# Decode steps in a new order, and the distance and mask tables made on GpSimd

## The chip, the cores and the metric

One core of a Trainium2 chip runs the whole program. The metric is the device time of one execution in microseconds (us). Engines: PE (TensorE), with PEld its weight loads; DVE (VectorE); ACT (ScalarE); POOL (GpSimd); SP, which here only issues DMAs.

## The reference

Local attention, a gated product network and a cosine network, one behind the other.

```python
def _attn_ref(q, k, v, n_global, n_local):      # 4 batches, 8 heads, 768 x 64
    scores = scale * np.matmul(q, k.transpose(0, 1, 3, 2))
    is_global = pos[None, :] < int(n_global)                     # 8 columns
    is_local = (rel >= 0) & (rel < int(n_local))                 # 96 back
    keep = is_global | is_local
    dist = np.where(is_global & ~is_local, float(n_local), np.abs(rel))
    scores = scores - slopes[:, None, None] * dist[None, :, :]
    scores = np.where(keep, scores, -1e9)
    return softmax(scores) @ v
def _moe_ref(x, w1, w2, w3, w_out):             # x 3072 x 512
    return ((x @ w1) * (x @ w2) @ w3) @ w_out
def _moe2_ref(x, w_in, w_out):                  # w_in 512 x 2048
    h = x @ w_in
    return (h * np.cos(h)) @ w_out
```

The weights come as 64-bit floats. They are read as pairs of 32-bit words, and the kernel builds 32-bit floats of them.

## The kernel before

**Decoding.** 72 weight pieces of 128x512 lie in one list: 32 of `w3`, `wo1`, `w1`, `w2` in mixed order with 8 more of `w1`, `w2` behind them, then 16 of `in` (w_in) and 16 of `o2` (the last w_out). The generator `decoder()` walks the list in iterations; iteration i works on piece i and on the four pieces ahead of it in the pipeline. The steps of one piece are: the load (`w_load`, 512 KB, on SP), the words (`dec_words`, two ACT passes, L338 and L339), the shift (`dec_shift`, DVE, L343), the sign (`dec_sign`, DVE, L347) and the sum (`dec_sum`, DVE, L355), which is the last to read the raw words. Pieces of `w1` and `w2` are then split for the three-pass product: the high part is a cast (`w_hi`, ACT, L419), the low part a subtraction (`w_lo`, DVE, L423). Pieces of `in` go through `combos`, pieces of `o2` are stored to `late_w`. The raw buffers number six for the first 30 pieces (`EARLY`) and three from then on. So a later load waits until the sum of the piece three before it has been made.

**What sets the order.** Each engine runs its instructions in the order in which the code was written; the main loops call `decode(n)`, which lets the generator run to its n-th next `yield`. The code has 21 such turns ahead of the first stage.

**First stage: 16 chunks c.** Each chunk multiplies one piece of `w3` with one of `wo1` (`wmm`, L890) and takes one attention tile n = c-1 through its steps: scores (`a_scores`, L582), bias and minimum (`a_max`, L610, DVE), exponential (`a_exp`, L621, ACT), sum and reciprocal (`a_norm`, L631 and L634, DVE), scaling (L640, ACT; later L642, POOL), transposition of the tile before (`a_transpose`, L649), copy (`a_tcopy`), values (`a_values`, L676). In the first four chunks ACT also scales the two tables `d0` and `dist` into a bias for each head (`bias_heads`, L521, L522).

**Second stage: 96 slots sl**, 8 rounds of 12, with attention tile n = sl + 14. Slots 0 to 7 of a round make two products (`up`), slots 8 to 11 one (`down`). The results of `down` go out through the single buffer `x2t` (`down_out`, an ACT copy, L748, then `down_store`, L751, on SP), one slot later: in the slots 9, 10, 11 and, in the next round, 0. Loads of `qk` and `v` for the attention stand first in a slot on SP. The third stage (L1001 and on) has no decoding.

**Tables.** `biases()` makes `d0` and `dist` from two iotas and from the two scalars n_local and n_global, which are fetched to all partitions (`nraw`, issued on ACT's queue).

Of the kernel before, what the change touches and what calls it, by code (L numbers as in the profile page):

```python
# [13 lines left out]
ALU = mybir.AluOpType  # L14
# [9 lines left out]
LOC, GLB = 96, 8  # L24
# [24 lines left out]
FAR = 2.0 ** 120  # L49
# [220 lines left out]
def fused(ctx, tc, a_qk, a_v, w3p, wo1p, w1p, w2p, winp, wo2p, n_global, n_local, out):  # L270
    nc = tc.nc
# [55 lines left out]
    def dec_words(key):  # L327
        r = raws[key]
        if key[0] in ("w3", "wo1"):

            tag = dest[key]
            kw = {"bufs": 4} if tag == "Wb" else {}
            if key[1] % 2 == 0:
                two[key[0]] = wts.tile([128, 2, 512], F32, tag=tag, name=key[0], **kw)
            x = xs[key] = two[key[0]][:, key[1] % 2, :]
        else:
            x = xs[key] = ring(key, "x", [128, 512], F32)
        nc.scalar.activation(x, r[:, :, 1].bitcast(F32), ACTF.Copy, scale=2.0 ** -112)  # L338
        nc.scalar.activation(r[:, :, 0], r[:, :, 0].bitcast(U32), ACTF.Copy, scale=2.0 ** -29)  # L339
# [98 lines left out]
    def scalars():  # L438
        raw = misc.tile([128, 2, 2], I32, name="nraw")
        for i, src in enumerate((n_local, n_global)):  # L440
            nc.scalar.dma_start(
                out=raw[:, i, :], in_=src.bitcast(I32).to_broadcast([128, 2])
            )
        yield
        lo = misc.tile([128, 2], F32, name="nlo")
        hi = misc.tile([128, 2], F32, name="nhi")
        ng = misc.tile([128, 2], F32, name="nneg")
        nv = misc.tile([128, 2], F32, name="nval")
        nc.vector.tensor_copy(out=lo, in_=raw[:, :, 0])
        nc.vector.tensor_copy(out=hi, in_=raw[:, :, 1])  # L450
        nc.vector.tensor_scalar(ng, lo, 0.0, None, ALU.is_lt)
        nc.vector.tensor_tensor(out=hi, in0=hi, in1=ng, op=ALU.add)
        nc.vector.scalar_tensor_tensor(
            out=nv, in0=hi, scalar=4294967296.0, in1=lo, op0=ALU.mult, op1=ALU.add
        )
        yield nv

    def biases(tp):

        rel = tp.tile([128, 128 + LOC], I32, name="rel")  # L460
        col = tp.tile([128, 128], I32, name="col")
# [11 lines left out]
        nc.vector.tensor_copy(out=dist[:, :nr], in_=rel)  # L473
        nc.vector.tensor_copy(out=colf, in_=col)
        steps = scalars()
        next(steps)
        yield
        nv = next(steps)
        nl, ng = nv[:, 0:1], nv[:, 1:2]
        yield nv  # L480
        nc.vector.tensor_scalar(lt[:, :nr], dist[:, :nr], nl, None, ALU.is_lt)
        yield
        nc.vector.scalar_tensor_tensor(
            out=keep[:, :nr], in0=dist[:, :nr], scalar=0.0, in1=lt[:, :nr],
            op0=ALU.is_ge, op1=ALU.mult,
        )
        yield
        nc.vector.tensor_scalar(gl, colf, ng, None, ALU.is_lt)
        yield
        nc.vector.tensor_copy(out=keep[:, nr:], in_=gl[:, :GLB])  # L490
        yield

        nc.vector.tensor_tensor(out=tmp, in0=gl, in1=keep[:, :128], op=ALU.mult)
        yield
        nc.vector.tensor_tensor(out=gl, in0=gl, in1=tmp, op=ALU.subtract)
        yield
        nc.vector.scalar_tensor_tensor(
            out=tmp, in0=dist[:, :128], scalar=nl, in1=gl, op0=ALU.subtract, op1=ALU.mult
        )
        yield  # L500
        nc.vector.tensor_tensor(out=d0, in0=dist[:, :128], in1=tmp, op=ALU.subtract)
        yield
        nc.vector.tensor_tensor(out=tmp, in0=gl, in1=keep[:, :128], op=ALU.add)
        yield

        nc.vector.tensor_scalar(tmp, tmp, -1.0, -FAR, ALU.add, ALU.mult)
        yield
        nc.vector.tensor_scalar(keep, keep, -1.0, -FAR, ALU.add, ALU.mult)
        yield
        nc.vector.tensor_scalar(dist[:, nr:], colf[:, :GLB], 0.0, nl, ALU.mult, ALU.add)  # L510
        yield
        nc.vector.tensor_tensor(out=d0, in0=d0, in1=tmp, op=ALU.add)
# [268 lines left out]
    with tc.manual_schedule():  # L781
# [8 lines left out]
        for o in "3A3A3A3A3A3A3A3ABBBBBBBB":  # L790
# [3 lines left out]
            else:  # L794
                n, m = ups.pop(0)
# [7 lines left out]
        tp = pool("tp", 1, side="right")  # L803
        EARLY = 30
# [6 lines left out]
        def decoder():  # L811


            n = len(dec)
            for i in range(2):
                w_load(*dec[i][:2])
            for i in range(n + 5):
                fast = i < EARLY
                k = [dec[i - l][0] if 0 <= i - l < n else None for l in range(5)]

                def ready(stage, lag):

                    for l in range(4, lag - 1, -1):
                        if k[l] and (stage, k[l]) not in done:
                            done.add((stage, k[l]))
                            if stage == "sum" or k[l] in xs and isinstance(dest[k[l]], str):
                                yield k[l]

                if fast and i + 2 < EARLY:
                    w_load(*dec[i + 2][:2])  # L830
                if k[0] and fast:
                    dec_words(k[0])
                if k[1]:
                    dec_shift(k[1])
                    yield
                for key in ready("sum", 2):
                    dec_sum(key)
                    yield
                for key in ready("hi", 3 if fast else 2):
                    w_hi(key, dest[key])  # L840
                for key in ready("lo", 4 if fast else 2):
                    w_lo(key, nc.vector)
                    yield
                if k[1]:
                    dec_sign(k[1])
                    yield
                if not fast:
                    for key in ready("sum", 1):
                        dec_sum(key)
                        yield  # L850
                    if k[1] and k[1][0] == "in" and k[1][1] % 2:
                        yield from combos(k[1][1] // 2)
                if EARLY <= i + 2 < n:
                    w_load(*dec[i + 2][:2])
                if k[0] and not fast:
                    dec_words(k[0])

        dest = {key: d for key, _, d in dec}
        done = set()
# [3 lines left out]
        def decode(n):  # L863
            for _ in range(n):
                next(steps_left, None)

        a_load_plain(0, nc.scalar)
        a_scores(0)
        nc.vector.memset(pt_ps, 0.0)
        steps_b = biases(tp)  # L870
        next(steps_b)
        make_identity(nc, ident)
        nv = dists = None
        for i in range(21):
# [4 lines left out]
            if i == 4:
                nv = next(steps_b)  # L880
            elif i >= 6:
                dists = dists or next(steps_b)
# [539 lines left out]
```

## Time and profile before

| what | value |
|---|---|
| three runs | median 1138.04 us (1134.91 to 1139.94) |
| profiled execution | 1136.57 us, of it the traced span 1134.7 us |
| granted TensorE clock, mean | 0.995 |
| PE busy | 1106.8 us (98%), 6034 matmuls |
| DVE busy | 777.9 us (69%) |
| ACT busy | 680.2 us (60%) |
| POOL busy | 81.5 us (7%) |
| DMA | 219.22 MB, mean 193 GB/s |

The 1.9 us between the execution and its span lie before the first and behind the last traced instruction. A busy share is an average over three stages; what a wait is worth is read in the stage where it stands.

### The profile page before, as it was taken

How to read it: one execution, taken by the hardware profiler on the slowest of the kernel's cores; microseconds unless marked ns; L12 is line 12 of the kernel's file. 1: busy time of each engine (PE TensorE's matmuls, PEld its weight loads, DVE VectorE, ACT ScalarE, POOL GpSimd, SP SyncE). 2: the span in 40 equal slices, each digit the busy share in tenths (PEclk: the TensorE clock that was granted, in tenths of full speed). 3: DMA queues.
4: the chain of work that ended last, by engine and by line, in shares of the span. 5: the costliest groups of instructions: out<-in, count | busy, mean ns of one | idle time of the engine just before them, and what ended most of it. 6: DMA issues, size and time to landing. Idle time of an engine off the chain costs nothing.

```text
span 1134.7 us, 17350 instructions
## 1 busy us (share of the span) xinstructions
PE 1106.8 (98%) x6034; PEld 957.3 (84%) x6034; DVE 777.9 (69%) x1661; ACT 680.2 (60%) x1370; POOL 81.5 (7%) x161
## 2 busy tenths in 40 slices
PE   5999999999999999999999999999999999999997
PEld 2455899999999999999999878888888888888886
DVE  7797666757667676896516588885677884777741
ACT  6897776756666666866624476654355562555531
POOL 0000001111111112122100001100000000000000
PEclk9899999999999999999999999999999999999999
DMA  8865355554555555776254736549375459474261
GB/s 279 250 223 162 123 183 168 176 170 160 178 159 165 189 178 186 265 244 204 59 176 140 274 128 233 213 167 367 129 299 189 136 197 381 152 283 167 75 234 65
DMA packets 86768, 219.22 MB, mean 193 GB/s; under 512 B 9616, under 2 KB 26256, under 8 KB 86672
## 3 DMA queue, kind: packets, MB, share of 16 engines
q1 hardware_dynamic: 86160, 217.70, 56.0%
q8 instruction: 50, 0.82, 0.3%
q14 instruction: 46, 0.38, 0.1%
q10 hardware_dynamic: 512, 0.32, 0.1%
HBM read 178.14 MB, written 39.85 MB: 192 GB/s over the span
## 4 chain that ended last, share of the span: by engine, by line
PE 88%; DVE 6%; ACT 3%; DMA 2%; issue 1%; ACTq 0%; SPq 0%; DVEq 0%
PE mm L432 32%; PE o_ps L432 23%; PE h_ps L432 19%; PE x_ps L676 4%; PE mm L890 4%; PE pt_ps L649 2%; PE pt_ps L651 1%; PE s_ps L594 1%; PE s_ps L590 1%; PE s_ps L582 1%; DVE x L347 1%; DMA nraw<-in_n_global 1%; DVE x L355 1%; DMA raw<-in_w3p 1%; DMA v<-in_a_v 1%
## 5 line engine op out<-in xcount | busy, mean ns | idle before, releaser
L432 PE MATMUL o_ps<-o,g 128*128 128x512 f32 x960 | 223.3, 389 | 0.0
L432 PEld LDWEIGHTS o_ps<-o,g 128*128 128x128 f32 x960 | 180.0, 188 | 37.5
L432 PE MATMUL mm<-xT,wA 128*128 128x384 f32 x768 | 148.5, 343 | 0.0
L432 PE MATMUL mm<-ab,W 128*128 128x384 f32 x768 | 147.1, 341 | 0.0
L432 PE MATMUL mm<-xT,wB 128*128 128x384 f32 x768 | 147.1, 341 | 0.0
L432 PE MATMUL h_ps<-T,piece 128*128 128x512 f32 x576 | 141.7, 389 | 0.1
L432 PEld LDWEIGHTS mm<-xT,wA 128*128 128x128 f32 x768 | 133.1, 190 | 2.2 <-issue 1.5
L432 PEld LDWEIGHTS mm<-ab,W 128*128 128x128 f32 x768 | 131.6, 188 | 2.7 <-issue 2.4
L432 PEld LDWEIGHTS mm<-xT,wB 128*128 128x128 f32 x768 | 131.7, 188 | 2.1 <-issue 2.1
L432 PEld LDWEIGHTS h_ps<-T,piece 128*128 128x128 f32 x576 | 107.9, 188 | 23.2 <-DVE gr L1234 0.5
L558 ACT CAST hh<-qk 128x720 fp32r<-128x720 f32 x74 | 58.8, 794 | 104.1 <-PE s_ps L594 95.9
L642 POOL TENSOR_SCALAR e<-e,st 128x232 f32<-128x232 f32 x148 | 74.5, 516 | 498.9 <-DVE st L634 438.4
L432 PE MATMUL h_ps<-B,piece 128*128 128x512 f32 x432 | 106.0, 389 | 0.0
L432 PEld LDWEIGHTS h_ps<-B,piece 128*128 128x128 f32 x432 | 81.0, 188 | 17.1 <-DVE vv L1234 0.4
L621 ACT ACTIVATE e<-e,top 128x232 f32<-128x232 f32 (+1 forms) x192 | 89.1, 466 | 3.4 <-DVE top L610 3.3
L610 DVE CUSTOM_DVE_ANT_0 e<-s_ps,bias 128x232 f32<-128x232 f32 (+1 forms) x192 | 65.2, 376 | 32.9 <-PE s_ps L594 28.5
L1126 ACT ACTIVATE r<-r 128x1024 f32<-128x1024 f32 x48 | 51.0, 1062 | 33.3 <-DVE r L1120 33.3
L890 PE MATMUL mm<-wo,w 128*128 128x512 f32 x128 | 64.5, 638 | 4.8 <-DVE wo L355 4.8
L719 DVE TENSOR_TENSOR a_sb<-mm,a_sb 128x384 f32<-128x384 f32 x64 | 35.5, 554 | 46.5 <-PE mm L432 46.3
L1120 DVE SCALAR_TENSOR_TENSOR r<-kt,r 128x1024 f32<-128x1024 int32 x48 | 58.8, 1225 | 1.5
L659 ACT COPY pt<-pt_ps 128x512 f32<-128x512 f32 x80 | 46.7, 584 | 14.0 <-PE pt_ps L651 14.0
L1139 ACT CAST g<-gr 128x512 fp32r<-128x512 f32 x48 | 29.0, 621 | 42.1 <-PE o_ps L432 42.1
(136 smaller groups left out, 1681.5 us busy)
## 6 DMA issues: line engine op xcount, KB each, us to landing
piece<-a_s SPq DMA_DIRECT2D x84, 512.0 KB, 5.6
o<-o2s SPq DMA_DIRECT2D x80, 512.0 KB, 5.8
qk<-in_a_qk SPq DMA_DIRECT2D x74, 360.0 KB, 3.3
a_s<-ap SPq DMA_DIRECT2D x56, 256.0 KB, 2.3
v<-in_a_v SPq DMA_DIRECT2D x96, 128.0 KB, 3.1
raw<-in_w3p SPq DMA_DIRECT2D x16, 512.0 KB, 5.6
raw<-in_winp SPq DMA_DIRECT2D x16, 512.0 KB, 4.3
raw<-in_wo2p SPq DMA_DIRECT2D x16, 512.0 KB, 4.6
```

The lines of the kernel that those rows point to most:

```text
L432: nc.tensor.matmul(ps, lhsT=l, rhs=r, start=first and i + e == 0, stop=last and i == n - 1 and e == 2, skip_group_check=more,)
L558: nc.scalar.copy(out=hh[n], in_=qk_raw[n])
L610: nc.vector.tensor_tensor_reduce(out=es[n][:, e, :w], in0=sp[:, e, :w], in1=bias[:, 2 * p + e, :], scale=-0.125, scalar=3.0e38, op0=ALU.ad ...
L621: nc.scalar.activation(es[n][:, e, :w], es[n][:, e, :w], ACTF.Exp, bias=top[:, n, e:e + 1], scale=-1.0, accum_out=sts[n][:, 0, e:e + 1],)
L642: nc.gpsimd.tensor_scalar(x, x, st[:, 1, e:e + 1], 1.0, ALU.mult, ALU.mult)
L659: nc.scalar.copy(out=pts[n].rearrange("p a b c -> p (a b c)"), in_=pt_ps.rearrange("p a b c -> p (a b c)"),)
L676: nc.tensor.matmul(x[e * 64:(e + 1) * 64, i * 128:(i + 1) * 128], lhsT=vt[:kk, c, e * 64:(e + 1) * 64], rhs=pt[:kk, e, c, :], start=c == 0 ...
L719: nc.vector.tensor_tensor(out=t, in0=mm_ps.pop("b"), in1=t, op=ALU.mult)
L890: nc.tensor.matmul(W_ps[m], lhsT=wt["w3", c][:, m * 128:(m + 1) * 128], rhs=wt["wo1", k], start=k == 0, stop=k == M1 - 1,)
L1120: nc.vector.scalar_tensor_tensor(out=self.r, in0=self.kt, scalar=-c, in1=self.h if c == C1 else self.r, op0=ALU.mult, op1=ALU.add,)
L1126: nc.scalar.activation(self.r, self.r, ACTF.Sin, scale=0.5)
L1139: nc.scalar.copy(out=t[:, 0, :], in_=src[:, m, :])
```

## The change

It has five parts. (1) The tables: all of `biases()` and `scalars()` runs on GpSimd, in one go ahead of the decoding, and the scalars are fetched first on ACT's queue, ahead of the first attention tile. (2) From piece 30 on, load and words stand at the head of an iteration instead of its end. (3) There the low part is made one iteration after the cast instead of in the same one. (4) The first two pieces are summed right after their signs. (5) Chunk 15 takes 2 decode turns in its last call instead of 5, and slots from 48 on take 3 instead of 4, as the slots from 8 on do.

```diff
@@ scalars
-        nc.vector.tensor_copy(out=lo, in_=raw[:, :, 0])
-        nc.vector.tensor_copy(out=hi, in_=raw[:, :, 1])
...
+        nc.gpsimd.tensor_copy(out=lo, in_=raw[:, :, 0])
+        nc.gpsimd.tensor_copy(out=hi, in_=raw[:, :, 1])
...
@@ biases
-        nc.vector.tensor_scalar(lt[:, :nr], dist[:, :nr], nl, None, ALU.is_lt)
-        yield
-        nc.vector.scalar_tensor_tensor(
-            out=keep[:, :nr], in0=dist[:, :nr], scalar=0.0, in1=lt[:, :nr],
-            op0=ALU.is_ge, op1=ALU.mult,
-        )
...
+        pool = nc.gpsimd
+        pool.tensor_copy(out=dist[:, :nr], in_=rel)
+        pool.tensor_copy(out=colf, in_=col)
+        pool.tensor_scalar(keep[:, :nr], dist[:, :nr], 0.0, None, ALU.is_ge)
...
+        pool.tensor_scalar(lt[:, :nr], dist[:, :nr], nl, None, ALU.is_lt)
+        pool.tensor_tensor(out=keep[:, :nr], in0=keep[:, :nr], in1=lt[:, :nr], op=ALU.mult)
...
+        pool.tensor_tensor(out=dist, in0=dist, in1=keep, op=ALU.add)
+        yield nv, d0, dist
@@ decoder
-                if fast and i + 2 < EARLY:
+                if i + 2 < n and fast == (i + 2 < EARLY):
                     w_load(*dec[i + 2][:2])
-                if k[0] and fast:
+                if k[0]:
                     dec_words(k[0])
                 if k[1]:
                     dec_shift(k[1])
...
-                for key in ready("lo", 4 if fast else 2):
+                for key in ready("lo", 4 if fast else 3):
                     w_lo(key, nc.vector)
                     yield
...
-                if not fast:
+                if not fast or i <= 2:
                     for key in ready("sum", 1):
                         dec_sum(key)
                         yield
-                    if k[1] and k[1][0] == "in" and k[1][1] % 2:
-                        yield from combos(k[1][1] // 2)
-                if EARLY <= i + 2 < n:
+                if not fast and k[1] and k[1][0] == "in" and k[1][1] % 2:
+                    yield from combos(k[1][1] // 2)
+                if fast and i + 2 >= EARLY:
                     w_load(*dec[i + 2][:2])
-                if k[0] and not fast:
-                    dec_words(k[0])
@@ first stage
+        steps_b = biases(tp)
+        next(steps_b)
         a_load_plain(0, nc.scalar)
...
+        nv, *dists = next(steps_b)
         for i in range(21):
             decode(1)
...
-            decode(2 if c < 8 else {14: 1, 15: 5}.get(c, 3))
+            decode(2 if c < 8 else {14: 1, 15: 2}.get(c, 3))
@@ second stage
-                decode(2 if sl < 8 or sl >= 48 else 1)
+                decode(2 if sl < 8 else 1)
```

**Place one: the start, on DVE and POOL.** DVE's instructions before, from the wait for the scalars on (`w_135` and `wo_140` are the first two pairs of pieces):

```order
L449 CAST nlo<-nraw 128x2
L450 CAST nhi<-nraw 128x2
L451 TENSOR_SCALAR nneg<-nlo 128x2
L452 TENSOR_TENSOR nhi<-nhi,nneg 128x2
L453 SCALAR_TENSOR_TENSOR nval<-nhi,nlo 128x2
L343 TENSOR_SCALAR w_135<-w_135 128x512
L355 ISA wo_140<-raw,wo_140 128x1024
L481 TENSOR_SCALAR lt<-dist,nval 128x224
L347 SCALAR_TENSOR_TENSOR w_135<-raw,w_135 128x512
L483 SCALAR_TENSOR_TENSOR keep<-dist,lt 128x224
```

DVE now, from its second instruction on:

```order
L343 TENSOR_SCALAR w_161<-w_161 128x512
L347 SCALAR_TENSOR_TENSOR w_161<-raw,w_161 128x512
L355 ISA w_161<-raw,w_161 128x1024
L343 TENSOR_SCALAR wo_166<-wo_166 128x512
L347 SCALAR_TENSOR_TENSOR wo_166<-raw,wo_166 128x512
L355 ISA wo_166<-raw,wo_166 128x1024
L343 TENSOR_SCALAR w_161<-w_161 128x512
L347 SCALAR_TENSOR_TENSOR w_161<-raw,w_161 128x512
```

and POOL now, the last twelve of the 21 that depend on the scalars:

```order
L485 COPY keep<-gl 128x8
L486 TENSOR_TENSOR tmp<-gl,keep 128x128
L487 TENSOR_TENSOR gl<-gl,tmp 128x128
L488 TENSOR_SCALAR tmp<-dist,nval 128x128
L489 TENSOR_TENSOR tmp<-tmp,gl 128x128
L490 TENSOR_TENSOR d_113<-dist,tmp 128x128
L491 TENSOR_TENSOR tmp<-gl,keep 128x128
L492 TENSOR_SCALAR tmp<-tmp 128x128
L493 TENSOR_TENSOR d_113<-d_113,tmp 128x128
L494 TENSOR_SCALAR keep<-keep 128x232
L495 TENSOR_SCALAR dist<-colf,nval 128x8
L496 TENSOR_TENSOR dist<-dist,keep 128x232
```

All 21 instructions of the tables left DVE; POOL has 24 for them, 21 of which stand behind the scalars in one chain.

**Place two: DVE between the first and the second stage,** from the low parts of the last product of the first stage (`W`) to the first slot's bias. Before:

```order
L899 TENSOR_TENSOR W<-mm,W 128x512 x4
L423 TENSOR_TENSOR wB<-x,wB 128x512
L347 SCALAR_TENSOR_TENSOR x<-raw,x 128x512
L355 ISA x<-raw,x 128x1024
L343 TENSOR_SCALAR x<-x 128x512
L423 TENSOR_TENSOR wB<-x,wB 128x512
L347 SCALAR_TENSOR_TENSOR x<-raw,x 128x512
L355 ISA x<-raw,x 128x1024
L343 TENSOR_SCALAR x<-x 128x512
L423 TENSOR_TENSOR wB<-x,wB 128x512
L610 ISA e,top<-s_ps,bias_89 128x232
```

Now:

```order
L875 TENSOR_TENSOR W<-mm,W 128x512 x4
L347 SCALAR_TENSOR_TENSOR x<-raw,x 128x512
L355 ISA x<-raw,x 128x1024
L343 TENSOR_SCALAR x<-x 128x512
L423 TENSOR_TENSOR wB<-x,wB 128x512
L347 SCALAR_TENSOR_TENSOR x<-raw,x 128x512
L355 ISA x<-raw,x 128x1024
L592 ISA e,top<-s_ps,bias_89 128x232
```

Six decode instructions stand there instead of nine. The first sum (L355) is that of the `w2` piece 5; the load of the `w1` piece 7 waits for it, and ACT's words of that piece now stand ahead of the first slot's exponential.

**Place three: SP in two slots of a round's end with `o2` pieces.** Before (slots 70 and 71):

```order
L537 DMA qk<-in_a_qk 128x720
L551 DMA v<-in_a_v 128x256
L359 DMA late_w<-x 128x512
L751 DMA x2s<-x2t 128x384
L325 DMA raw<-in_wo2p 128x1024
L537 DMA qk<-in_a_qk 128x720
L551 DMA v<-in_a_v 128x256
L359 DMA late_w<-x 128x512
L751 DMA x2s<-x2t 128x384
L359 DMA late_w<-x 128x512
```

Now (slots 69 to 72 each read like this):

```order
L519 DMA qk<-in_a_qk 128x720
L533 DMA v<-in_a_v 128x256
L325 DMA raw<-in_wo2p 128x1024
L733 DMA x2s<-x2t 128x384
L359 DMA late_w<-x 128x512
```

The raw load moved ahead of the store of `x2t`. It waits for the sum of the piece three before it, which DVE makes as the last decode step of the same slot.

## Rows read from the trace of the kernel before

**Rows 1.** Page, part 4: the chain that ended last, share by engine.

```profile
PE 88%; DVE 6%; ACT 3%; DMA 2%; issue 1%; ACTq 0%; SPq 0%; DVEq 0%
```

**Rows 2.** Waits of PE: engine, line, releaser; us in all, times, longest.

```profile
PE mm L890 <- DVE wo L355: 4.8, 1, 4.8
PE pt_ps L649 <- ACT e L640: 4.6, 2, 2.4
PE x_ps L676 <- DMA v<-in_a_v: 4.2, 3, 1.8
```

**Rows 3.** Waits of DVE for ACT's words.

```profile
DVE x L343 <- ACT x L338: 22.6, 28, 2.1
```

**Rows 4.** Timeline, ACT and PE, 20 to 34 us: start, us, instruction, [idle before].

```profile
20.79 0.31 ACT L521 ACTIVATE bias<-d 128x128 f32<-128x128 f32 x1 [0.72 <-DVE d L512]
21.70 0.40 ACT L522 ACTIVATE bias<-dist 128x232 f32<-128x232 f32 x1 [0.60 <-DVE dist L514]
...
29.10 0.67 ACT L338 ACTIVATE w<-raw 128x512 f32<-128x512 f32 x1 [0.79 <-DMA raw<-in_w3p]
...
33.16 5.54 PE L890 MATMUL mm<-wo,w 128*128 128x512 f32 x8
```

**Rows 5.** Windows: us, PE, PEld, DVE, ACT, POOL busy (x), PEclk, DMA share, GB/s.

```profile
20.00:30.00 10.00, 6.50 (x18) 2.68 (x16) 10.00 (x29) 7.89 (x23) 0.00 (x0) 1.00 0.90 265
```

**Rows 6.** Timeline, DVE: first and last of 19 table instructions behind the scalars.

```profile
10.35 0.17 DVE L449 CAST nlo<-nraw 128x2 f32<-128x2 int32 x1 [1.54 <-DMA nraw<-in_n_global]
...
21.28 0.39 DVE L514 TENSOR_TENSOR dist<-dist,keep 128x232 f32<-128x232 f32 x1
```

**Rows 7.** Groups of POOL by form: busy us, mean ns of one.

```profile
L642 POOL TENSOR_SCALAR e<-e,st 128x232 f32<-128x232 f32 x124 | 64.8, 535 | 451.8 <-DVE st L634 394.8 <-ACT pt L659 36.0 <-PE s_ps L594 12.2
L642 POOL TENSOR_SCALAR e<-e,st 128x128 f32<-128x128 f32 x24 | 9.7, 417 | 47.1 <-DVE st L634 43.6 <-ACT pt L659 3.5
L423 POOL TENSOR_TENSOR wB<-raw,wB 128x512 fp32r<-128x512 f32 x4 | 5.8, 1438 | 150.3 <-ACT wB L419 150.3
```

**Rows 8.** Timeline, POOL: the same pair twice.

```profile
453.46 0.90 POOL L642 TENSOR_SCALAR e<-e,st 128x232 f32<-128x232 f32 x2 [4.28 <-DVE st L634]
...
466.16 1.59 POOL L642 TENSOR_SCALAR e<-e,st 128x232 f32<-128x232 f32 x2 [6.17 <-DVE st L634]
```

**Rows 9.** DVE's sums, L355: ns min/median/max of one.

```profile
L355 DVE CUSTOM_DVE_ANT_0 x<-raw,x x48: 668/685/834, 48.8 to 525.3; 128x1024 uint16<-128x1024 uint16 x48
```

**Rows 10.** Timeline, PE, the first nine slots: scores of tiles 14, 21, 22.

```profile
103.19 1.05 PE L582 MATMUL s_ps<-hh 64*128 64x232 f32 x4
...
114.89 0.33 PE L649 MATMUL pt_ps<-ident,e 128*128 128x128 f32 x1 [2.43 <-ACT e L640]
...
152.71 1.05 PE L582 MATMUL s_ps<-hh 64*128 64x232 f32 x4
...
158.41 0.27 PE L590 MATMUL s_ps<-hh 128*128 128x232 f32 x1
```

**Rows 11.** Timeline, DVE, SP and ACT, end of the first stage.

```profile
103.52 2.48 DVE L899 TENSOR_TENSOR W<-mm,W 128x512 fp32r<-128x512 f32 x4 [0.61 <-ACT W L898]
...
107.99 0.33 SPq L325 DMA_DIRECT2D raw<-in_w1p  x1
...
112.37 0.49 ACT L621 ACTIVATE e<-e,top 128x232 f32<-128x232 f32 x1 [1.08 <-DVE top L610]
```

**Rows 12.** DMA issues, 90 to 130 us: KB each, median us to landing.

```profile
raw<-in_w1p SPq DMA_DIRECT2D x3, 512.0 KB, 3.5
```

**Rows 13.** Timeline, SP, ACT and PE, 505 to 516 us.

```profile
505.58 0.38 SPq L325 DMA_DIRECT2D raw<-in_wo2p  x1
506.05 0.38 SPq L751 DMA_DIRECT2D x2s<-x2t  x1
...
511.56 0.48 ACT L748 COPY x2t<-mm 128x384 f32<-128x384 f32 x1 [2.88 <-DMA x2s<-x2t]
...
515.52 0.66 PE L676 MATMUL x_ps<-pt,v 128*64 128x128 f32 x8 [1.83 <-DMA v<-in_a_v]
```

More of the change, by code (lines that the diff above doesn't have):

```diff
@@ L448, in scalars @@
         nv = misc.tile([128, 2], F32, name="nval")
-        nc.vector.tensor_copy(out=lo, in_=raw[:, :, 0])
-        nc.vector.tensor_copy(out=hi, in_=raw[:, :, 1])
-        nc.vector.tensor_scalar(ng, lo, 0.0, None, ALU.is_lt)
-        nc.vector.tensor_tensor(out=hi, in0=hi, in1=ng, op=ALU.add)
-        nc.vector.scalar_tensor_tensor(
-            out=nv, in0=hi, scalar=4294967296.0, in1=lo, op0=ALU.mult, op1=ALU.add
-        )
+        nc.gpsimd.tensor_copy(out=lo, in_=raw[:, :, 0])
+        nc.gpsimd.tensor_copy(out=hi, in_=raw[:, :, 1])
+        nc.gpsimd.tensor_scalar(ng, lo, 0.0, None, ALU.is_lt)
+        nc.gpsimd.tensor_tensor(out=hi, in0=hi, in1=ng, op=ALU.add)
+        nc.gpsimd.tensor_scalar(hi, hi, 4294967296.0, None, ALU.mult)
+        nc.gpsimd.tensor_tensor(out=nv, in0=hi, in1=lo, op=ALU.add)
         yield nv
@@ L472, in biases @@
         nr = 128 + LOC
-        nc.vector.tensor_copy(out=dist[:, :nr], in_=rel)
-        nc.vector.tensor_copy(out=colf, in_=col)
+        own = slice(0, 128)
         steps = scalars()
@@ L477, in biases @@
         yield
+        pool = nc.gpsimd
+        pool.tensor_copy(out=dist[:, :nr], in_=rel)
+        pool.tensor_copy(out=colf, in_=col)
+        pool.tensor_scalar(keep[:, :nr], dist[:, :nr], 0.0, None, ALU.is_ge)
         nv = next(steps)
         nl, ng = nv[:, 0:1], nv[:, 1:2]
-        yield nv
-        nc.vector.tensor_scalar(lt[:, :nr], dist[:, :nr], nl, None, ALU.is_lt)
-        yield
-        nc.vector.scalar_tensor_tensor(
-            out=keep[:, :nr], in0=dist[:, :nr], scalar=0.0, in1=lt[:, :nr],
-            op0=ALU.is_ge, op1=ALU.mult,
-        )
@@ L487, in biases @@
[L487 to L512, printed above, removed]
@@ L513, in biases @@
-        yield
-        nc.vector.tensor_tensor(out=dist, in0=dist, in1=keep, op=ALU.add)
-        yield d0, dist
+        pool.tensor_scalar(lt[:, :nr], dist[:, :nr], nl, None, ALU.is_lt)
+        pool.tensor_tensor(out=keep[:, :nr], in0=keep[:, :nr], in1=lt[:, :nr], op=ALU.mult)
+        pool.tensor_scalar(gl, colf, ng, None, ALU.is_lt)
+        pool.tensor_copy(out=keep[:, nr:], in_=gl[:, :GLB])
+        pool.tensor_tensor(out=tmp, in0=gl, in1=keep[:, own], op=ALU.mult)
+        pool.tensor_tensor(out=gl, in0=gl, in1=tmp, op=ALU.subtract)
@@ new lines, in biases @@
+        pool.tensor_scalar(tmp, dist[:, own], nl, None, ALU.subtract)
+        pool.tensor_tensor(out=tmp, in0=tmp, in1=gl, op=ALU.mult)
+        pool.tensor_tensor(out=d0, in0=dist[:, own], in1=tmp, op=ALU.subtract)
+        pool.tensor_tensor(out=tmp, in0=gl, in1=keep[:, own], op=ALU.add)
+        pool.tensor_scalar(tmp, tmp, -1.0, -FAR, ALU.add, ALU.mult)
+        pool.tensor_tensor(out=d0, in0=d0, in1=tmp, op=ALU.add)
+        pool.tensor_scalar(keep, keep, -1.0, -FAR, ALU.add, ALU.mult)
+        pool.tensor_scalar(dist[:, nr:], colf[:, :GLB], 0.0, nl, ALU.mult, ALU.add)
@@ L869, in fused @@
         nc.vector.memset(pt_ps, 0.0)
-        steps_b = biases(tp)
-        next(steps_b)
         make_identity(nc, ident)
-        nv = dists = None
+        nv, *dists = next(steps_b)
         for i in range(21):
@@ L878, in fused @@
                 a_load_v(0)
[L879 to L882, printed above, removed]
         W_ps = {}
```

## The prediction

> **What bounds the kernel now.** I read the chain that ended last first: 88% of it is PE, so an edit on DVE, ACT or SP can only pay where PE waits [rows 1]. Then the waits of PE, and the reader is to see how short that list is: 4.8 us for the first sum at the very start, 4.6 us for the scaled tile, twice, and 4.2 us for `v` loads, three times [rows 2]. Against it stand 22.6 us in 28 waits of DVE for ACT's words [rows 3]. The change takes most of those 28 away, but in nearly all of them PE had work, so they are no part of the sum. Three places are left, and I read the timelines there.
>
> The start, up to 33.16 us, where PE begins the fourth chunk and then works without a pause for some 60 us [rows 4]. What holds it back is ACT, which goes through its words in program order. It stood 0.72 us for `d0`, 0.60 us for `dist` and 0.79 us for a raw piece [rows 4].
>
> The first slots. From the scores of tile 14 to those of tile 22 pass 55.22 us, eight slots. The last of them, without values, takes 5.70 us [rows 10]. Two of the eight have values as well, some 1.5 us each (an estimate: 24 matmuls a slot, of which a group of eight took 0.66 us [rows 13], so 2.0 if none overlaps, and I take 1.5). So 55.22 - 45.6 - 3.0 = 6.6 us are lost, and 2.43 us of that is one wait, at 114.89 [rows 10].
>
> The slots with `o2` pieces, 1.33 of them a slot, where the three waits for `v` lie. The last is 1.83 us at 515.52. Just before it ACT stood 2.88 us for the store of `x2t`, which SP had issued right behind a raw load [rows 13].
>
> **The start: -1.0 us.** DVE loses 21 instructions, 19 of them behind the scalars, 0.17 to 0.39 us each, and with them the 1.54 us in which it stood for the scalars [rows 6]. DVE was busy in the whole of 20 to 30 us [rows 5], so raw loads, which wait for its sums, are issued earlier. Two things cap this. The DMA engines were at 0.90 in that window [rows 5]: in ten microseconds data can come 1.0 us earlier, no more. And ACT's waits there are 2.1 us in all [rows 4]. So the gain lies between 0 and 2.1 us if the tables come in time; I take 1.0, the nearer row.
>
> Do they? POOL's chain is not in the trace, so I build it from its three rows [rows 7]. One-input operations cost 0.42 us on 128 columns and 0.54 on 232, so about 0.27 us fixed. The two-input one took 1.44 us on 512 columns; less the fixed part that is 2.3 ns a column, so 0.56 us on 128, 0.78 on 224 and 0.80 on 232. Of the 21 instructions behind the scalars eight are tiny (2.2 us), five one-input (2.3), eight two-input (six at 0.56, one at 0.78, one at 0.80: 5.0). Together 9.5 us, `d0` 1.6 us ahead of `dist`. The scalars landed by 10.35 us as the last of three transfers on ACT's queue [rows 6]; now they are first. I put them at 7.5 us, with 5 and 10.3 as ends.
>
> POOL and DVE also get in each other's way. One pair of scalings took 0.90 us, the same pair 1.59 us in a stretch with two decode instructions of DVE beside it, and DVE's sums, 0.685 us at the median, reach 0.834 [rows 8, 9]. So one POOL instruction loses up to (1.59 - 0.90) / 2 = 0.35 us, 21 of them 7.3 us if DVE never pauses. It pauses while it waits for words, so I take half, 3.7 us. `dist` is then ready at 7.5 + 9.5 + 3.7 = 20.7 us, `d0` at 19.1. ACT comes to `d0` at 20.79 - 0.72 = 20.1 and to `dist` 0.3 us later, so it stands some 0.3 us instead of 1.3. That fits the 1.0.
>
> The Trainium skill speaks against this edit (SBUF — State Buffer, "SBUF: two separate sides"): the port pair that GpSimd and VectorE share is an exclusive lock, held for a whole instruction, and the loser blocks fully. The trace agrees that POOL waits [rows 8], but DVE's sums lost 0.15 us at most [rows 9], less than a third of the instruction that POOL ran; taken at its word, the rule makes the lock rival below of this term.
>
> The first two sums made at once cost and bring nothing: the first product now waits for the first tile's scores, whose load became the last of the three on ACT's queue, due by 10.3 us, and the products are early for ACT anyway. If that load came later than 12 us, the start would lose the difference.
>
> **The first slots: -1.3 us.** Six decode instructions instead of nine stand between the `W` low parts and the first slot's bias, so the bias of tile 14 comes some 2.5 us earlier on DVE. I don't count that for the wait at 114.89, because something else is late next. The `W` low parts end at 106.0 us [rows 11]. Behind them come one sign and one sum, 0.69 us each [rows 9]: 107.3. Only then can SP issue the raw load that before went out at 107.99 [rows 11], and one of 512 KB lands 3.5 us later [rows 12]: 110.9. Since words now stand early, ACT makes that piece's words ahead of the exponential of tile 14: three passes with the cast behind them, 0.67 us each [rows 4], so the exponential starts at 112.9. Before it started at 112.37 [rows 11]. So this wait stays. Of the other 4.2 us of the 6.6, which come from DVE waiting for words and casts, I take 30%, since ACT is as full as before. The ends are +0.5 (the wait a little longer, nothing else gained) and -5.5 us (load in time, nearly all gone).
>
> **The `o2` slots: -1.0 us.** Sixteen slots with one piece each take the place of twelve with 1.33. DVE has one step of 0.69 us less a slot, and a quarter of the weight bytes less goes ahead of `v`. That would take most of the three 1.4 us waits. But a raw load now stands ahead of the store of `x2t` on SP and waits for the last decode step of the same slot. Queued behind it are that store, the `late_w` store, `qk` and `v`. In slots 69 to 72 this happens four times in a row: store late, next `down_out` on ACT late, exponential late, sum late, next load late. One such wait was 2.88 us [rows 13]; PE's own slack swallows the first, and of the next three I let 3.2 us reach PE, with 0 and 9 (three times 3) as ends. 4.2 becomes 3.2.
>
> **Slots 11, 12, 35, 36, 59 and 60: +1.3 us.** The same store stands behind a raw load in slots 10 and 11, 34 and 35, 58 and 59. Two in a row are mostly swallowed; I take 0.4 us for each of the three pairs, with 0 and 4.5 us (1.5 each) for all as ends. The move of `late_w` and the later end of the decoding (slot 81 instead of 72) cost nothing: the last round's loads begin in slot 84.
>
> **Sum.** -1.0 - 1.3 - 1.0 + 1.3 = -2.0 us. The profiled execution took 1136.57 us, 1134.7 of it span; the change would make it 1134.6. It lies 1.5 us below the median of the three runs, so for a median I give 1138.04 - 2.0 = 1136.0 us.
>
> **Rivals.**
>
> *Clear gain, 0.31.* The early load lands ahead of ACT, and the stores of `x2t` find a free queue, so that the slots keep PE's pace: start -1.0, first slots -5.0, `o2` -4.0, pairs 0: -10 us, 1128.0. For it speaks that the DMA engines are far from full outside the start, and that the median landing is 3.5 us [rows 12], less than a slot's 5.70 [rows 10]. Against it, place three: the wait is for the sum, not for bandwidth.
>
> *The lock, 0.09.* Every POOL instruction and every decode instruction exclude each other wholly, from either side. POOL's 9.5 us then become DVE time as well, `dist` is ready at 10.3 + 9.5 + 7.3 = 27.1 us, 5.4 after the 21.70 of before [rows 4]; less the 0.79 us that ACT stood anyway, the start loses 4.6 instead of gaining 1.0: 1141.6. It decides from `dist` at 22 us on, one microsecond for one. By the rule of the Trainium skill (SBUF — State Buffer) quoted above it would come out so.
>
> *The chain of stores, slower, 0.10.* The mechanism of the `o2` term at its ends: 9 us of waits instead of 4.2 (+4.8), the three pairs at 4.5, start -1.0, first slots -1.3: +7.0, 1145.0. It decides when the store of `x2t` lands later than some 3 us into the next slot in each of the runs of slots; the 2.88 us wait shows that it can [rows 13].
>
> *It doesn't do what it says.* Words early means only that ACT, not DVE, waits for the raw piece. Then the first slots gain nothing: 1137.3, inside the forecast.
>
> **Chances.** The forecast has 0.50, its own range 1133 to 1140. 0.5% of the median, 5.7 us, is about what a measurement can tell. Faster by more (below 1132.3): the clear gain and a little of the forecast's edge, 0.33. Slower by more (above 1143.7): the chain and a little of the lock, 0.12. The rest, 0.55. The range for eight in ten is 1127 to 1143.5.
>
> **What would show it.** Start: POOL's last table instruction at 20 to 22 us, ACT's first bias within 0.5 us of 20.4, the fourth chunk's product at 32 us. First slots: a raw load at 107 to 108 us and the transposition of tile 14 still waiting 2 us or more; if that wait is gone, the first-slot term is wrong. `o2`: ACT waiting for `x2s` in slots 70 to 73, raw loads each at the end of their slot, and waits for `v` of some 3 us in all. A prediction that is wrong will most likely be so there: if ACT shows no wait for `x2s`, the clear gain is right, and if it shows one in slots 11, 35 and 59 that PE answers, the chain.

## The result, and the profile after

Six runs of the changed kernel have a median of 1145.47 us (1142.96 to 1146.50) against 1137.37 us (1134.91 to 1139.94) of the kernel before: ratio 1.0066, 95% interval 1.0048 to 1.0084. It became slower by 8 us, where 2 us less were forecast. The profiled execution took 1145.51 us, its span 1143.6 us.

Page of the changed kernel, part 4, which answers to [rows 1]:

```profile
PE 84%; DMA 5%; ACT 4%; DVE 3%; issue 2%; POOL 1%; SPq 0%; ACTq 0%; POOLq 0%; DVEq 0%
```

PE's share fell from 88 to 84% and that of transfers rose from 2 to 5%. Waits of PE and then of ACT in the changed kernel, which answer to [rows 2] (its line numbers behind the tables are 18 to 24 lower; us in all, times, longest):

```profile
PE s_ps L564 <- DMA hh<-in_a_qk: 11.5, 2, 10.6
PE pt_ps L631 <- POOL e L624: 5.5, 4, 1.7
PE pt_ps L631 <- ACT e L622: 5.2, 2, 2.9
PE x_ps L658 <- DMA v<-in_a_v: 2.0, 2, 1.7
...
ACT x2t L730 <- DMA x2s<-x2t: 30.7, 10, 5.2
```

Before, the first and the last of these rows were:

```profile
PE s_ps L582 <- DMA hh<-in_a_qk: 7.0, 2, 5.4
...
ACT x2t L748 <- DMA x2s<-x2t: 4.4, 2, 2.9
```

The row of PE is for attention tiles, above all the first one, for which PE now waits until 10.57 instead of 5.41 us. It was the longest in PE's list before, and [rows 2] left it out. The row of ACT is the one that grew most: nine of the ten waits for the store of `x2t`, 29.3 us, lie in the slots with decoding, where before there was one of 2.88 us [rows 13]; the tenth, of 1.4 us, comes later and was there before too. DVE's row of waits for the words of [rows 3] is gone from its list, and PE has new waits for POOL's scaling, four times.

**Where the time went.** PE starts the scores of every tile in the same place of its program. Their start, from the timelines of PE, splits the 8.6 us up to slot 81; the difference of two neighbouring columns is what a stretch cost.

| us at which PE starts the scores of tile | 3 | 14 | 22 | 28 | 52 | 76 | 86 | 95 |
|---|---|---|---|---|---|---|---|---|
| slot | first stage | 0 | 8 | 14 | 38 | 62 | 72 | 81 |
| before | 39.07 | 103.19 | 158.41 | 192.05 | 325.74 | 459.44 | 520.85 | 571.65 |
| changed | 40.20 | 104.33 | 158.17 | 193.57 | 329.07 | 464.97 | 521.47 | 580.28 |
| changed less before | +1.13 | +1.14 | -0.24 | +1.52 | +3.33 | +5.53 | +0.62 | +8.63 |

So: start +1.1, first slots -1.4, three pairs of slots +1.8, +1.8 and +2.2, slots 62 to 72 -4.9, slots 72 to 81 +8.0. Behind slot 81 another 0.3 us (spans 1143.6 and 1134.7).

**The chain of stores.** Timeline of the changed kernel, SP, ACT, DVE and PE in slots 71 to 74 (start, us, instruction, [idle before]):

```profile
516.73 0.39 SPq L733 DMA_DIRECT2D x2s<-x2t  x1
...
525.78 0.33 SPq L325 DMA_DIRECT2D raw<-in_wo2p  x1
526.20 0.38 SPq L733 DMA_DIRECT2D x2s<-x2t  x1
...
521.39 0.48 ACT L730 COPY x2t<-mm 128x384 f32<-128x384 f32 x1 [3.67 <-DMA x2s<-x2t]
521.77 0.49 ACT L603 ACTIVATE e<-e,top 128x232 f32<-128x232 f32 x1
...
524.79 0.17 DVE L613 TENSOR_SCALAR st<-st 128x2 f32<-128x2 f32 x1
...
525.08 0.67 DVE L355 CUSTOM_DVE_ANT_0 x<-raw,x 128x1024 uint16<-128x1024 uint16 x1
...
530.51 0.48 ACT L730 COPY x2t<-mm 128x384 f32<-128x384 f32 x1 [5.02 <-DMA x2s<-x2t]
...
526.13 0.33 PE L631 MATMUL pt_ps<-ident,e 128*128 128x128 f32 x1 [1.68 <-POOL e L624]
...
526.91 3.70 PE L432 MATMUL mm<-xT,wA 128*128 128x384 f32 x12
...
539.50 0.66 PE L658 MATMUL x_ps<-pt,v 128*64 128x128 f32 x8 [1.74 <-DMA v<-in_a_v]
540.09 3.92 PE L432 MATMUL mm<-xT,wA 128*128 128x384 f32 x12
```

Read by time it is a ring. ACT's copy (521.39) comes late, so the exponential (521.77), DVE's step ahead of the reciprocal (524.79) and the sum behind it (525.08) come late. Only then can SP issue the raw load (525.78), and behind it the store (526.20). The next copy into the one buffer waits for that store and runs at 530.51: 9.1 us from copy to copy, where a slot takes 5.70 [rows 10].

PE answers twice. It waits 1.68 us for the scaled tile, and the next 12 matmuls take 3.70 us, where such a group takes 2.35 with the clock at its upper level. Window of the changed kernel over this wait (columns as in rows 5):

```profile
520.00:530.00 10.00, 8.32 (x40) 7.44 (x39) 5.16 (x14) 4.09 (x10) 1.15 (x2) 0.83 0.52 171
```

The granted clock of this stretch is 0.83, a mix of the two levels. Behind the wait for `v` at 539.50 it is the same again: 1.74 us of wait, and 3.92 us for the next 12 matmuls. The two waits and the 1.35 + 1.57 us of slow matmuls are 6.3 of the 8.0 us; the rest lies in the same two slots.

**The first slots.** Timeline of the changed kernel, SP, ACT and PE; it answers to [rows 11] and the wait in [rows 10]:

```profile
108.63 0.33 SPq L325 DMA_DIRECT2D raw<-in_w1p  x1
...
112.09 0.66 ACT L338 ACTIVATE x<-raw 128x512 f32<-128x512 f32 x1 [2.88 <-DMA raw<-in_w1p]
...
113.72 0.48 ACT L603 ACTIVATE e<-e,top 128x232 f32<-128x232 f32 x1
...
116.06 0.33 PE L631 MATMUL pt_ps<-ident,e 128*128 128x128 f32 x1 [2.35 <-ACT e L622]
```

ACT stood 2.88 us for the raw piece, made its words and its cast, and then the exponential. The wait of PE stayed (2.43 us before).

**The start.** Timeline of the changed kernel, POOL, DVE, PE and ACT:

```profile
8.64 0.18 POOL L449 CAST nlo<-nraw 128x2 f32<-128x2 int32 x1 [5.37 <-DMA nraw<-in_n_global]
...
22.49 0.73 POOL L496 TENSOR_TENSOR dist<-dist,keep 128x232 f32<-128x232 f32 x1
...
22.61 1.16 DVE L355 CUSTOM_DVE_ANT_0 w<-raw,w 128x1024 uint16<-128x1024 uint16 x1
...
12.41 9.83 PE L866 MATMUL mm<-wo,w 128*128 128x512 f32 x16
...
33.98 5.86 PE L866 MATMUL mm<-wo,w 128*128 128x512 f32 x8
...
6.02 0.66 ACT L338 ACTIVATE w<-raw 128x512 f32<-128x512 f32 x1 [2.51 <-DMA raw<-in_w3p]
```

The last row before:

```profile
4.40 0.66 ACT L338 ACTIVATE w<-raw 128x512 f32<-128x512 f32 x1 [0.67 <-DMA raw<-in_w3p]
```

`dist` was ready at 23.2 us, 14.6 us behind the first table instruction that depends on the scalars. ACT's words began 1.6 us later than before, and ACT came to the first bias at 21.81 us, where it had come at 20.07. The fourth chunk began at 33.98 instead of 33.16 us [rows 4].

### The profile page after: what moved, and what is told of

The parts are those of the page before. It is cut to its first block, busy times and chain, and to the rows that moved or that the text cites. A ratio compares the mean times of both kernels' runs of the same rounds, so it can differ in the third digit from the quotient of the medians.

```text
span 1143.6 us, 17329 instructions
## 1 busy us (share of the span) xinstructions
PE 1112.0 (97%) x6034; PEld 959.9 (84%) x6034; DVE 773.5 (68%) x1640; ACT 677.9 (59%) x1370; POOL 93.5 (8%) x185
## 4 chain that ended last, share of the span: by engine, by line
PE 84%; DMA 5%; ACT 4%; DVE 3%; issue 2%; POOL 1%; SPq 0%; ACTq 0%; POOLq 0%; DVEq 0%
PE mm L432 29%; PE o_ps L432 23%; PE h_ps L432 19%; DMA x2s<-x2t 3%; PE x_ps L658 3%; PE mm L866 3%; PE pt_ps L631 2%; ACT e L603 1%; PE pt_ps L633 1%; PE s_ps L564 1%; PE s_ps L576 1%; PE s_ps L572 1%; DMA raw<-in_w2p 1%; DMA nraw<-in_n_global 1%; DVE x L355 1%
## 5 line engine op out<-in xcount | busy, mean ns | idle before, releaser
L432 PE MATMUL mm<-xT,wA 128*128 128x384 f32 x768 | 151.7, 348 | 0.1
L432 PEld LDWEIGHTS mm<-xT,wA 128*128 128x128 f32 x768 | 136.0, 194 | 2.6 <-issue 1.5
L432 PEld LDWEIGHTS h_ps<-T,piece 128*128 128x128 f32 x576 | 108.0, 188 | 23.2 <-DVE gr L1210 0.5
L624 POOL TENSOR_SCALAR e<-e,st 128x232 f32<-128x232 f32 x148 | 71.8, 497 | 489.4 <-DVE st L616 428.6
L631 PE MATMUL pt_ps<-ident,e 128*128 128x128 f32 x192 | 46.9, 278 | 10.9 <-POOL e L624 5.5
L673 DVE TENSOR_TENSOR xT<-x_ps,xT 128x384 fp32r<-128x384 f32 x32 | 17.8, 557 | 55.0 <-ACT xT L672 55.0
```

The lines of the kernel that those rows point to most:

```text
L432: nc.tensor.matmul(ps, lhsT=l, rhs=r, start=first and i + e == 0, stop=last and i == n - 1 and e == 2, skip_group_check=more,)
L624: nc.gpsimd.tensor_scalar(x, x, st[:, 1, e:e + 1], 1.0, ALU.mult, ALU.mult)
L631: nc.tensor.transpose(pt_ps[:, e, 0, :], e_t[:, e, :128], ident)
L673: nc.vector.tensor_tensor(out=t[:, 1, :], in0=x, in1=t[:, 0, :].bitcast(F32), op=ALU.subtract)
```

## The experiments

Three theories on the slots: A, the harm goes through the one buffer of `x2t`; B, it goes through `qk` and `v`, which stand behind the waiting load on SP; C, slots with decoding are simply too full.

**The store on ACT's queue.**

```diff
-        nc.sync.dma_start(out=x2s[m, :, j * TB:(j + 1) * TB], in_=x2t.pop((j, m)))
+        nc.scalar.dma_start(out=x2s[m, :, j * TB:(j + 1) * TB], in_=x2t.pop((j, m)))
```

> The changed kernel, with the stores of x2t issued on ACT's queue instead of SP's, so that they no longer stand behind the raw load. Theory A (single buffer): the harm of the early load goes through x2t's one buffer, 5.7 us on PE in slots 11 to 14, 35 to 38 and 59 to 62 and 8.0 us in slots 72 to 75. Then all 13.7 us go: 1145.5 - 13.7 = 1131.8 us (1129 to 1135), and ACT's copy waits less than 3 us in all for x2s in the second stage instead of 29. Theory B (queue): the harm goes through qk and v, which still stand behind the waiting load on SP; then the time stays at 1142 to 1146 and PE still waits in slots 73 to 75.

Measured: 1133.20 us (1131.62 to 1134.84), ratio to the kernel before 0.9969 (0.9956 to 0.9982). Tile 95 starts at 566.32 us, 14.0 us ahead of the changed kernel, of which 13.2 lie in the pairs and behind slot 72 (5.8 and 7.4). Waits of PE and of ACT in this run:

```profile
PE x_ps L658 <- DMA v<-in_a_v: 0.4, 1, 0.4
...
ACT hh L540 <- DMA qk<-in_a_qk: 16.7, 11, 2.4
ACT x2t L730 <- DMA x2s<-x2t: 13.2, 4, 6.7
```

A holds, B falls. `qk` still comes late (16.7 us of ACT's waits against 7.7), and PE hardly feels it. In the slots where ACT had its 29.3 us of waits for `x2s`, none is left. One number of A was wrong: ACT waits 13.2 us for `x2s` in all, not under 3. One of the four waits ends at 577.03 us, in slot 83, the other three from 625.54 on, in and behind the last round; why the stores on ACT's queue are late there stays open.

**The raw load late.** Load behind the sums again, words early:

```diff
-                if i + 2 < n and fast == (i + 2 < EARLY):
+                if fast and i + 2 < EARLY:
                     w_load(*dec[i + 2][:2])
...
-                if fast and i + 2 >= EARLY:
+                if EARLY <= i + 2 < n:
                     w_load(*dec[i + 2][:2])
```

> The changed kernel, with the raw load from piece 30 on back at the end of an iteration (words stay at its head). Theories A (single buffer of x2t) and B (qk and v behind the load on SP) both expect 1131.8 us (1129 to 1136), since no load waits any more for a sum of its own slot. Theory C (the slots with decoding are simply too full on DVE or ACT): it stays at 1142 to 1146. If the time lies well above e1's, loads that come a slot later make ACT wait for raw pieces, which would stand in ACT's waits as more than 6 us for raw.

Measured: 1130.52 us (1129.66 to 1130.91), ratio 0.9940 (0.9926 to 0.9954). Tile 95 at 565.68. C falls: the place of the load alone is worth 14.6 us up to there between this run and the changed kernel. Waits of PE:

```profile
PE s_ps L564 <- DMA hh<-in_a_qk: 11.6, 2, 10.7
PE pt_ps L631 <- ACT e L622: 5.4, 2, 3.0
PE x_ps L658 <- DMA v<-in_a_v: 0.2, 1, 0.2
```

**The tables on DVE again** (parts of the diff on `scalars`, `biases` and their calls undone).

> The changed kernel with the tables on DVE and the scalars behind the first attention tile, as before the change. Theory D (the tables on GpSimd cost the start 0.8 us at the fourth chunk, 1.1 us from tile 3 on): the fourth chunk's product starts at 33.2 us again, tile 14's scores at 103.2. Rival E (the two sums made at once are what delays it): 33.9 and 104.3 stay. Time, one look: 1144.4 under D, 1145.5 under E.

Measured, one run: 1146.13 us, above both theories. The fourth chunk starts at 32.85 us, as D has it, but tile 3 at 39.67 and tile 14 at 103.79, halfway between D and E. So the tables on GpSimd cost about half of the 1.1 us, if anything; this isn't shown, since five runs with the changed start have tile 3 at 39.15 to 40.20 us. PE's rows of this run show why DVE alone doesn't cure it:

```profile
12.33 9.90 PE L888 MATMUL mm<-wo,w 128*128 128x512 f32 x16 [4.96 <-DVE wo L355]
```

The first product waits until 12.33 us for a sum of DVE, although the first two sums now stand early: DVE waits for the scalars ahead of the second one.

**The scalars fetched second,** tables on GpSimd:

```diff
-        steps_b = biases(tp)
-        next(steps_b)
         a_load_plain(0, nc.scalar)
         a_scores(0)
+        steps_b = biases(tp)
+        next(steps_b)
```

> The changed kernel with the scalars fetched behind the first attention tile on ACT's queue; the tables stay on GpSimd. Theory F (the fetch ahead is what costs: the DMA engines moved 180 to 190 GB/s at 2 to 5 us instead of 221 to 407): the fourth chunk's product comes at 33.3 us or earlier. Rival G (GpSimd's chain of 14.6 us from the scalars to dist sets the start): the scalars land about 1.7 us later, dist is ready at some 24.9 us instead of 23.2, and the product comes at 34.5 to 35.5 us.

Measured, one run: 1146.61 us. Rows of PE's timeline, and one of ACT's waits:

```profile
9.21 5.26 PE L866 MATMUL mm<-wo,w 128*128 128x512 f32 x8 [2.01 <-DVE wo L355]
...
32.22 0.68 PE L631 MATMUL pt_ps<-ident,e 128*128 128x128 f32 x2 [8.08 <-ACT e L622]
```

```profile
ACT bias L503 <- POOL d L493: 4.5, 1, 4.5
```

Both theories have a half. The fetch ahead did hold the first product: it now starts at 9.21 us instead of 12.41, since the first tile lands 4.5 us after its issue instead of 8.9. But POOL's chain then sets the start: `dist` is ready at 25.8 us, ACT stands 4.5 us for `d0`, the fourth chunk starts at 36.33, later than either theory had it, and tile 3 at 42.05, 1.9 us later than in the changed kernel. ACT's first words come at 4.59 us again, so it was the fetch ahead that had delayed them.

**One piece a slot, alone, in the kernel before.**

```diff
-                decode(2 if sl < 8 or sl >= 48 else 1)
+                decode(2 if sl < 8 else 1)
```

> The kernel before, with one edit of the change alone: slots from 48 on take 3 decode turns instead of 4, so one o2 piece a slot instead of 1.33. Theory H (the rate of pieces made the three waits for v): on PE some 5 us go between slots 60 and 72 (4.9 was gained there by the changed kernel), and no store chain comes, since loads stand at the end of an iteration: 1136.4 - 5 = 1131.5 us (1130 to 1133). Rival I (the early words or the later low parts did it): at most 1 us goes.

Measured: 1131.61 us (1131.51 to 1131.77), ratio 0.9956 (0.9940 to 0.9973). Tile 76 starts 0.2 us earlier than before, tile 86 5.6 us. H holds. The list of PE's waits has no row for `v` any more:

```profile
PE s_ps L582 <- DMA hh<-in_a_qk: 6.8, 2, 5.7
PE mm L890 <- DVE wo L355: 4.8, 1, 4.8
PE pt_ps L649 <- ACT e L640: 4.8, 2, 2.4
PE x_ps L676 <- ACT pt L659: 0.7, 2, 0.4
```

**The load late and 1.33 pieces a slot** (the edit of the run before, undone in the run with the load late).

> The changed kernel with the raw load at the end of an iteration (as in the run with the load late) and with 4 decode turns a slot from slot 48 on, as before the change. Theory H: the waits for v between slots 60 and 72 come back, 1130.5 + 5 = 1135.5 us (1134 to 1137). Rival I: it stays within 1 us of 1130.5.

Measured: 1139.81 us (1136.57 to 1143.72), ratio 1.0029 (1.0007 to 1.0050). H again in the main, but 4.3 us over its forecast of 1135.5. PE's three pauses ahead of the values come back in the same places (477.11, 495.66 and 514.75 us, 4.2 us in all), but only one of them ends with `v`; the other two end with ACT. What comes on top would be ACT's waits for raw pieces, 2.3 us in the run with the load late; that is not shown by itself:

```profile
ACT x L338 <- DMA raw<-in_wo2p: 11.2, 6, 5.2
```

With early words a load that is late holds ACT instead of DVE.

**Words late too** (part 2 undone whole).

```diff
-                if k[0]:
+                if k[0] and fast:
                     dec_words(k[0])
...
                 if EARLY <= i + 2 < n:
                     w_load(*dec[i + 2][:2])
+                if k[0] and not fast:
+                    dec_words(k[0])
```

> The changed kernel with its second part undone whole: from piece 30 on load and words both at the end of an iteration. Theory J (words early bring the 1.4 us of the first slots): PE's lead over the run with the load late is lost between the slots 0 and 6, 1.4 us, so 1132 us. Rival K (the later low parts and the shorter call in chunk 15 bring them): it stays at 1130.5, and the wait for tile 14's scaling gets shorter than 2.35 us, since the words of the w1 piece no longer stand ahead of its exponential. No store chain in either.

Measured: 1127.09 us (1126.71 to 1127.14), ratio 0.9916 (0.9899 to 0.9932). J falls outright: the early words did not bring the 1.4 us, they cost 4.4 in slots 0 to 7, and 3.4 in the time. K had the wait right, and its time 3.4 us too high. Tile 14 starts at 104.14 us and tile 22 at 153.50, 5.9 us less for these eight slots than before. PE's waits, and the window of 110 to 120 us:

```profile
PE s_ps L564 <- DMA hh<-in_a_qk: 11.2, 2, 10.6
PE pt_ps L631 <- ACT e L622: 2.7, 1, 2.7
PE x_ps L658 <- ACT pt L646: 1.3, 1, 1.3
```

```profile
110.00:120.00 10.00, 10.00 (x71) 8.93 (x71) 8.24 (x25) 8.79 (x24) 0.00 (x0) 1.00 0.67 172
```

Tile 14's wait is gone, and the clock of this stretch is 1.00; in the changed kernel it was 0.84, and the 12 matmuls behind the wait took 3.89 us.

**The scalars' step two turns later,** tables on DVE, load late, words early:

```diff
-            if i == 4:
+            if i == 6:
                 nv = next(steps_b)
-            elif i >= 6:
+            elif i >= 7:
                 dists = dists or next(steps_b)
```

> The run with the load late, with the tables on DVE and the scalars behind the first attention tile, but with the scalars' step two decode turns later than before the change (behind turn 6 instead of 4), so that DVE makes the first two sums before it waits for the scalars. Theory L (what held the first product is DVE waiting for the scalars in front of the second sum, and what then holds the start is the tables): first product at 9.2 to 9.6 us, the tables no later than before (dist by 22 us), and tile 14's scores at 102.5 to 103.2: 1130.5 - 1 = 1129.5 us. Rival M (the DMA engines set the pace to 33 us): the first product comes early but tile 14 stays at 103.2 to 103.8 and the time at 1130.5.

Measured: 1128.51 us (1127.90 to 1129.09), ratio 0.9930 (0.9914 to 0.9947). The first product starts at 9.54 us, `dist` is ready at 21.4, and tile 14 starts at 101.48, a little better than L said; M falls:

```profile
9.54 9.72 PE L888 MATMUL mm<-wo,w 128*128 128x512 f32 x16 [2.23 <-DVE wo L355]
```

**Both: words late, scalars later.** That is parts 3, 4 and 5 of the change without its parts 1 and 2.

> Parts 3, 4 and 5 of the change alone (low parts an iteration later, the first two sums at once, fewer decode turns in chunk 15 and from slot 48 on), with load, words, tables and scalars as before the change, but the scalars' step two decode turns later. If the terms add: the start -1.7 as in the run with the later scalars, first slots -5.9 and slots 60 to 72 -5.4 as in the run with the words late: 1136.5 - 13 = 1123.5 to 1124.5 us. Rival: the earlier start only waits more at tile 14 or in the first slots, and the time stays at 1127.

Measured: 1125.65 us (1124.82 to 1126.39), ratio 0.9901 (0.9883 to 0.9919): the best kernel here, 10.8 us under the kernel before. The terms nearly add: tile 95 starts 12.1 us earlier than before, where 13 were expected. What is short there is the start, where tile 3 came at 38.32 us and not at 37.35 (the next two runs, with the same start, have 38.75 and 38.86, so a start repeats to within some 1.5 us only). Another 1.5 us are lost at the very end: the span ends 6.7 us after the last store is issued, against 5.2 before. All of PE's waits that are left lie ahead of 33 us:

```profile
PE s_ps L582 <- DMA hh<-in_a_qk: 5.9, 1, 5.9
PE pt_ps L649 <- ACT e L640: 4.0, 1, 4.0
PE mm L890 <- DVE wo L355: 1.8, 1, 1.8
PE x_ps L676 <- ACT pt L664: 1.5, 1, 1.5
```

**Chunk 15 with 5 turns,** and **the low part in its cast's iteration,** each in the kernel that joins both:

```diff
-            decode(2 if c < 8 else {14: 1, 15: 2}.get(c, 3))
+            decode(2 if c < 8 else {14: 1, 15: 5}.get(c, 3))
```

```diff
-                for key in ready("lo", 4 if fast else 3):
+                for key in ready("lo", 4 if fast else 2):
```

> The run that joins both, with chunk 15's last call at 5 decode turns again. Theory N (the nine decode instructions of DVE ahead of tile 14's bias make the wait of 2.4 us and the low clock behind it): PE waits 2 us or more for tile 14 again and 4.4 us come back, 1128.4 us. Rival O (the later low parts take that wait away): it stays at 1124.0, with no such wait.

> The run that joins both, with the low part made in the iteration of its cast again (DVE waits for ACT's cast then). Theory O (the later low parts bring the small steps of slots 1 to 6, 1.4 us, and perhaps tile 14's wait): 1125.4 us, or 1129.8 if the wait comes back too. Rival N (the shorter call alone does it all): 1124.0.

Measured: 1126.89 us (1125.89 to 1128.18), ratio 0.9910 (0.9892 to 0.9928), and 1129.19 us (1128.70 to 1130.49), ratio 0.9932 (0.9914 to 0.9949). From tile 14 to tile 22 pass 49.35 us in the joined kernel, 50.36 with the long call, 52.84 with the low part soon; with the long call one wait for `v`, 1.2 us, also comes back at the end of the `o2` pieces. N falls: the long call costs 1.0 us there, not 4.4. O holds for the larger part: the later low part brings 3.5 us. Neither alone brings back a wait of 2.4 us for tile 14, so with words late either of the two takes that wait away.

## Why the prediction was wrong

The terms below are those of the two profiled executions, whose spans differ by 8.9 us (the medians by 8.1).

**The pairs of slots** (+1.3 predicted, +5.8 measured) failed at "Two in a row are mostly swallowed; I take 0.4 us for each". Each pair cost 1.8 to 2.2 us, above the end of 1.5 that I had set. The first wait was mostly swallowed, but the second is longer and reached PE: ACT stood 1.64 and then 4.85 us at 179.37 and 188.22, and in the same way in the other two pairs. A wait lengthens the next, since the load that the store stands behind waits for a sum that the wait itself made late. The two runs that take the store or the load out of this ring show it.

**The `o2` slots** (-1.0 predicted, +3.1 measured) were two terms that I had netted into one. One piece a slot took the three waits for `v` away, as I had said, and brought 4.9 us, more than their 4.2. The chain then cost 8.0 where I let "3.2 us reach PE". The mechanism and its order (store late, copy late, exponential late, sum late, next load late) were as written. The waits that reached PE were 3.4 us, close to the 3.2. The size failed because I priced a wait of PE at its own length: 2.9 of the 8.0 us are matmuls at the lower clock behind the two waits, and 1.7 more were lost beside them. The lower clock isn't needed for it: in the run with the scalars second the same ring left three waits of 1.69, 1.68 and 2.18 us with the granted clock at 1.00 throughout, and slots 72 to 80 still took 6.7 us more than before. The rival named the chain of stores had +7.0 us and 1145.0, with a tenth of the chance. Its mechanism was right; that its number came so near is in part luck, since it had +4.8 for these slots, +4.5 for the pairs and -1.0 for the start, where +3.1, +5.8 and +1.1 came.

**The start** (-1.0 predicted, +1.1 measured, +0.1 to +1.1 in the five runs with it) failed at "raw loads are issued earlier". The instructions that left DVE were not what held the first product; the wait for the scalars ahead of the second sum was before, and the first tile was now, which landed 8.9 us after its issue behind the two fetches of the scalars. The raw loads came later and not earlier: ACT's first words began at 6.02 instead of 4.40 us, a price of the fetch ahead that the sum had put at nothing. "If that load came later than 12 us, the start would lose the difference" was no safe bound: the load came at 10.6 us, and the first product 0.3 us later than before. `dist` came at 23.2 us, not 20.7, since the scalars came at 8.64 instead of 7.5 us and POOL's chain took 14.6 us, worked out as 9.5 and 3.7. How the 1.1 us divide between the fetch and the tables is not shown. And "the first two sums made at once cost and bring nothing" holds only as long as something else holds the first product: with the scalars out of the way it starts at 9.2 to 9.7 us.

In that chain both engines lost. Between 14.7 and 23.8 us nine decode instructions of DVE took 0.1 to 0.5 us longer than elsewhere, 2.1 us in all, the longest 1.16 against 0.685 us. POOL's 128x8 step (L495) took 1.20 us beside decode instructions, and 0.27 us in the run with the scalars second, where DVE stood idle. By the Trainium skill (SBUF — State Buffer, "SBUF: two separate sides") whichever of the two engines starts first keeps the shared port pair for its whole instruction, and the other blocks fully. The trace agrees in direction, with these numbers. It does not decide whether the block is full, since an instruction that comes in the middle of another would wait only for the rest of it, and five of DVE's nine losses are of 0.25 to 0.27 us. The prediction's largest loss of DVE, 0.15 us [rows 9], was too small a guide.

**The first slots** (-1.3 predicted, -1.4 measured) were right in number and in the wait. The load went out at 108.63 and landed 3.5 us later, the exponential came at 113.72 (112.9 predicted, and the start's 1.1 on top), and the wait of 2.35 us stayed. What the prediction did not see is what follows from it: with words late, that wait and its clock, 4.4 us, are gone. The gain was put down to DVE no longer waiting for words and casts; the early words brought nothing, and the later low part and the shorter call brought 5.9 us, of which the early words took 4.4 back. So the number fits in part by luck. The later end of the decoding cost next to nothing, as forecast: 0.3 us behind slot 81.

## What to carry to other kernels

Before a load is moved ahead in a queue, look for what stands behind it there: if it waits for work of its own slot, everything behind it inherits the wait, and a store of a single buffer closes that into a ring, whose waits grow. Price a wait of PE by how much longer its slots took, not by its own length alone, and net two effects of opposite sign only after each has its own price. Parts of one change can cancel: here three of the five parts and one moved step bring 10.8 us, and the other two, the early load above all, cost more than that.

## What the hardware showed unexpectedly

Short waits of PE differ in what they cost behind them. In the changed kernel the next 12 matmuls took 2.33 to 2.35 us after waits of 1.10, 1.31 and 1.42 us (190.76, 326.28 and 462.18 us), and 3.70, 3.92 and 3.89 us after 1.68, 1.74 and 2.35 us. The length of the wait does not decide it: in the run with the scalars second they took 2.35 to 2.36 us after 1.68, 1.69 and 2.18 us, and in the kernel before, behind the wait of 1.83 us at 515.52 [rows 13], 2.37 us:

```profile
516.12 2.37 PE L432 MATMUL mm<-ab,W 128*128 128x384 f32 x12
```

What PE did shortly before each wait was not varied, so the runs give no rule for it.

Two fetches of 1 KB each, the scalars spread over all partitions, ahead of the first tile on the same queue made that tile's 180 KB land 8.9 us after its issue instead of 4.6 (4.5 in the run with the scalars second).
